# Part of w_o's first rows by GpSimd's queue instead of a half row set aside: one decode step on one core

## The chip, the cores and the metric

The kernel runs on one core of a Trainium2 chip. The metric is the device time of one execution in microseconds (us); the time before is the median of three runs. A profile is one execution recorded by the hardware profiler. Its span goes from the first to the last instruction and is a little shorter than the time of a run.

The core has TensorE (PE, with weight loads as PEld), VectorE (DVE), ScalarE (ACT), GpSimd (POOL) and SyncE (SP), and 16 DMA engines that all of them share. In the kernel, SP issues nearly all transfers.

## The reference

One decode step: attention over a cache and a gated feed-forward block, both fed by the same normalised row, and added.

```python
def _A_ref(x, k_cache, v_cache, wq, wo):          # H, Sk, Dh = 32, 16384, 128; D = 576
    q = (x @ wq).reshape(B, Sq, H, Dh).transpose(0, 2, 1, 3)
    p = _softmax(einsum("bhqd,bhkd->bhqk", q, k_cache) * Dh ** -0.5)
    o = einsum("bhqk,bhkd->bhqd", p, v_cache)
    return o.transpose(0, 2, 1, 3).reshape(B, Sq, H * Dh) @ wo
def _B_ref(x, w_gate, w_up, w_down):              # Df = 4608
    return (_gelu(x @ w_gate) * (x @ w_up)) @ w_down
xn = _layernorm(x)
return x + _A_ref(xn, ...) + _B_ref(xn, ...)
```

All data is float32. K and V of one head are 8 MB each, 32 heads make 537 MB; the weights add 50 MB. Each byte is used once.

## The kernel before, in words

**Order by hand.** `Plan` keeps one list of operations for each engine; `op` and `dma` (L54 to L66) append to it, with the semaphores that the operation waits for. What stands earlier in an engine's list runs earlier on it. `dma` adds 16 to a semaphore when the whole transfer has landed; `then` lets an engine raise a semaphore itself once what it is given has come.

**Stages.** SP loads the three input projections first (w_q, w_gate, w_up, L208 to L300). Then come 32 heads: SP loads K into two buffers in turn and V into one (L405 to L424), VectorE multiplies K by the query and sums, TensorE multiplies by V. SP's list runs ahead: a load is issued as soon as the buffer it overwrites has been read (semaphores `s_kf` for K, `s_vf` for V).

**The end.** With the last heads, free K buffers take the weights of the two output projections. w_down has 36 rows a partition (`FT`), w_o has 32 (`WT`); a "row" here is 576 floats (2304 bytes) in each of 128 partitions, since both are laid out as `(p t) f -> p (t f)`. In SP's list the order is: 28 rows of w_down (L427), the last V (L428), 8 rows of w_down (L429), and then w_o in pieces of 12, 6, 6 and six single rows (`WO_CUTS`, L444 to L449). The first 18 rows of w_o go behind w_down's last 8 into one buffer (`wo0`), free when the last K has been read (`s_kf`, 2). The others wait for VectorE's adds over w_down's first 28 rows (`k_w0`).

Row 31 is split. Its right part (columns 320 to 575, `LEFT` is 320) is loaded early, after the first 18 rows, by eight transfers of 16 KB (L450 to L454): the 128 partitions are laid as two halves beside each other in 64 partitions (`aside`), and one transfer fills eight partitions that are four apart. Row 30 comes in two pieces, right part then left, and the left part of row 31 is last (L456).

**The output.** Attention's 4096 values stand as a column per row of w_o in `oT` (L468). Three routes sum the product into the result:

- VectorE multiplies rows 0 to 10 (`ON_DVE`) by their column and adds them into `wacc`, where w_down's rows and x are already (L470 to L474). Before row 8 it adds the half row set aside, in two halves (L471 to L473); the second needs half of `oT`'s last column moved to the lower partitions (`o31`, L469).
- TensorE sums rows 11 to 25 into `acc` (L491 to L494). VectorE adds `acc` and `wacc` into `part` (L495).
- TensorE sums rows 26 to 31 and `part` over the partitions into one row of results, in three pieces `pair[0]`, `pair[1]` and `third` (L496 to L507). Three copies bring them to `osb`, and SP stores it (L508 to L512).

Of the kernel before, what the change touches and what calls it, by code (L numbers as in the profile page):

```python
# [13 lines left out]
P = 128  # L14
H, SK, DH = 32, 16384, 128
D, DF = 576, 4608
# [7 lines left out]
FT = DF // P  # L24
WT = HD // P
S0 = 32512
SLOT = 4 * N * DH
WD1 = 28
WO1 = 18
# [2 lines left out]
LAST = 6  # L32
SIDE = 160
LEFT = 2 * SIDE
ASIDE = 8
SEL = 396


class Plan:
# [14 lines left out]
    def op(self, e, fn, *deps, sig=None, by=1):  # L54
        if e in ("dve", "act", "pool"):
            deps += (self.last.get(e),)
        sig = sig or self.own[e]
        self.count[sig.name] = self.count.get(sig.name, 0) + by
        self.q[e].append((deps, fn, sig, by))
        if sig is self.own[e]:  # L60
            self.last[e] = sig, self.count[sig.name]
        return sig, self.count[sig.name]

    def dma(self, e, out, in_, *deps, sem=None):
        sem = sem or self.sem(f"d{len(self.count)}")
        return self.op(e, lambda g: g.dma_start(out, in_), *deps, sig=sem, by=16)  # L66
# [65 lines left out]
def plan(nc, pl, x, k_cache, v_cache, wq, wo, wg, wu, wd, out):  # L132
    op, dma = pl.op, pl.dma
# [4 lines left out]
    wov = wo.rearrange("(p t) f -> p (t f)", t=WT)  # L138
# [5 lines left out]
    def small(name, shape, where=None):  # L144
        if where is None:
            size = 4
            for n in shape[1:]:
                size *= n
            where = place[name] = top[0]
            top[0] += -(-size // 32) * 32  # L150
            assert top[0] <= S0, (name, top)
        return nc.alloc_sbuf_tensor_at(name, shape, F32, offset=where).ap()

    def big(name, floats, where):
        assert where + 4 * floats <= 3 * SLOT
        return nc.alloc_sbuf_tensor_at(name, [P, floats], F32, offset=S0 + where).ap()
# [10 lines left out]
    pm, nm, nb, pe = small("pm", [P, 1]), small("nm", [1, 1]), small("nb", [P, 1]), small("pe", [P, N])  # L167
    ls, o4 = small("ls", [P, H + 1]), small("o4", [P, 512])
    oall, oT = small("oall", [P, H + 1]), small("oT", [P, WT])
    o31 = small("o31", [P // 2, 1])  # L170
    gu, hT = small("gu", [P, 2, FT]), small("hT", [P, FT])
    sel = small("tmp", [P, 3 * SEL])
    over = place["tmp"]
# [6 lines left out]
    B, A, C = 0, SLOT, 2 * SLOT  # L180
# [5 lines left out]
    vt = big("vt", N * DH, C)  # L186
    wd0, wd1 = big("wd0", WD1 * D, B), big("wd1", (FT - WD1) * D, A)
    wo0, wo1 = big("wo0", WO1 * D, A + 4 * (FT - WD1) * D), big("wo1", (WT - WO1) * D, B)
    aside = big("aside", 2 * (D - LEFT), A + 4 * (FT - WD1 + WO1) * D)[: P // 2]

    def banks(*shapes):
        with ExitStack() as s:
# [6 lines left out]
    s_hs, s_pm, s_nm, s_p, s_o4, s_v = (pl.sem(n) for n in ("hs", "pm", "nm", "p", "o4", "v"))  # L199
    s_pq, s_pt, s_pb, s_pv, s_pc = (pl.sem(n) for n in ("pq", "pt", "pb", "pv", "pc"))  # L200
    s_qb, s_ol, s_kf, s_vf, s_d, s_a = (pl.sem(n) for n in ("qb", "ol", "kf", "vf", "d", "a"))
    s_kh, s_aside = pl.sem("kh"), pl.sem("aside")
    s_k = [pl.sem(f"k{i}") for i in range(2)]


# [20 lines left out]
    for i in range(2):  # L226
        k = op("dve", lambda g, i=i: g.bn_stats(st[:, i, :], xrow[:, i * HALF : (i + 1) * HALF]), d_x)
    k = op("dve", lambda g: g.bn_aggr(mv, st), k)
    k = op("act", lambda g: g.activation(std, mv[:, 1:2], AF.Sqrt, bias=eps[:1], scale=1.0), k, c_eps)
    k = op("dve", lambda g: g.reciprocal(rstd, std), k)  # L230
# [3 lines left out]
    for j in range(DJ):  # L234
        k = op("pe", lambda g, j=j: g.transpose(px[:, j : j + 1], xm[:, j, :], ones[:1, :1]), k_xn, c_ones)
    k = op("pe", lambda g: g.transpose(px[:, DJ : DJ + 1], xd.rearrange("o d s -> o (d s)"), ones[:1, :1]), k_xd)
    k = op("dve", lambda g: g.tensor_copy(xp, px[:, : DJ + 1]), k)
# [14 lines left out]
    def add(out, w, c, into, *deps):  # L252
        return op("dve", lambda g: g.scalar_tensor_tensor(out, w, c, into, op0=ALU.mult, op1=ALU.add), *deps)  # L253
# [47 lines left out]
    _, g_k, k = rows(gw, gt, d_g, [(0, DF // 4, 0)], lambda: select(qsel, 384, 8, 1))  # L301
# [5 lines left out]
    k = op("act", lambda g: g.activation(qb[0], pqb[:, 0, :DH], AF.Copy), (s_q0, 2))  # L307
# [6 lines left out]
    k = op("pool", lambda g: g.tensor_mul(t1, g_, g_), k_g)  # L314
    k = op("pool", lambda g: g.tensor_scalar(t1, t1, 0.044715, 1.0, op0=ALU.mult, op1=ALU.add), k)
    k = op("pool", lambda g: g.tensor_mul(t1, t1, g_), k)
    k = op("act", lambda g: g.activation(th, t1, AF.Tanh, scale=0.7978845608028654), k)
    k = op("pool", lambda g: g.tensor_scalar(t2, th, 0.5, 0.5, op0=ALU.mult, op1=ALU.add), k)
    k_t = op("pool", lambda g: g.tensor_mul(t2, t2, g_), k)
    k = op("act", lambda g: g.activation(sel.rearrange("p (b c) -> p b c", b=3), pw[:, :, :SEL], AF.Copy), (s_w, 3), k_g, k_t)  # L320
    op("act", lambda g: pick(g, 1), (s_q0, 3), sig=s_hs)
    v = sel[:, : 32 * FT].rearrange("p (r t) -> p r t", r=32)
    k = op("pool", lambda g: g.tensor_mul(v, v, m32[:, :32].unsqueeze(2).to_broadcast([P, 32, FT])), k, c_m32)
    for r in (16, 8, 4, 2, 1):
        o = v[:, :r, :] if r > 1 else u_.unsqueeze(1)
        k = op("pool", lambda g, o=o, r=r: g.tensor_tensor(o, v[:, :r, :], v[:, r : 2 * r, :], op=ALU.add), k)  # L326
    k = op("pool", lambda g: g.tensor_mul(hT, t2, u_), k)
    k = op("pool", lambda g: g.memset(wacc, 0.0), k)
# [104 lines left out]
    o_sum = wacc.rearrange("p a f -> p (a f)")  # L433

    def down(lo, hi, w, dep, k):
        for t in range(lo, hi):
            r, c = w[:, (t - lo) * D : (t - lo + 1) * D], hT[:, t : t + 1]
            k = add(o_sum, r, c, o_sum, dep, k, k_h)
        return k

    k_w0 = down(0, WD1, wd0, d_wd0, None)
    k_w1 = down(WD1, FT, wd1, d_wd1, k_w0)
    d_wo, lo = [], 0
    for n in WO_CUTS:  # L444
        w, base, dep = (wo0, 0, (s_kf, 2)) if lo < WO1 else (wo1, WO1, k_w0)
        c = w[:, (lo - base) * D : (lo - base + n) * D]
        d = dma("sp", c, wov[:, lo * D : (lo + n) * D], dep)
        d_wo += [(c[:, i * D : (i + 1) * D], d) for i in range(n)]
        lo += n  # L449
        if lo == WO1:  # L450
            last = wo.rearrange("(s r t) f -> t r s f", s=2, t=WT)[WT - 1]
            for r in [b + j for b in (0, 32) for j in range(4)]:
                to = aside[r : r + 29 : 4].rearrange("r (s f) -> r s f", s=2)
                d_aside = dma("sp", to, last[r : r + 29 : 4, :, LEFT:], dep, sem=s_aside)  # L454
    assert len(d_wo) == WT - 2
    for t, a, b in ((WT - 2, LEFT, D), (WT - 2, 0, LEFT), (WT - 1, 0, LEFT)):  # L456
        c = wo1[:, (t - WO1) * D + a : (t - WO1) * D + b]
        d_wo.append((c, dma("sp", c, wov[:, t * D + a : t * D + b], k_w0)))


    k = op("pe", lambda g: g.matmul(pqb[:, 0, :H], ones, ls[:, :H], start=True, stop=True))
    k = op("dve", lambda g: g.reciprocal(rl, pqb[:, 0, :H]), k)  # L462
    k = op("dve", lambda g: g.tensor_mul(oexp, oall[:, :H].unsqueeze(2).to_broadcast([P, H, 4]),  # L463
                                         rl.unsqueeze(2).to_broadcast([P, H, 4])), k, k_o)
    k = op("pe", lambda g: g.transpose(pt[:, 0, :P], oexp.rearrange("p h a -> p (h a)"), ident), k)  # L465
    k = op("dve", lambda g: g.tensor_mul(ot, pt[:, 0, :P].rearrange("p (a t) -> p a t", a=4),  # L466
                                         m4.unsqueeze(2).to_broadcast([P, 4, 32])), k, c_m4)
    k_oT = op("dve", lambda g: g.tensor_reduce(oT, ot.rearrange("p a t -> p t a"), axis=AX.X, op=ALU.add), k)  # L468
    k_o31 = op("dve", lambda g: g.tensor_copy(o31, oT[P // 2 :, WT - 1 :]), k_oT)  # L469
    for t in ON_DVE:  # L470
        for i, c in enumerate((oT[: P // 2, WT - 1 :], o31) if t == ASIDE else ()):  # L471
            to = o_sum[: P // 2, LEFT:]
            k_w1 = add(to, aside[:, i * (D - LEFT) : (i + 1) * (D - LEFT)], c, to, d_aside, k_w1, k_o31)  # L473
        k_w1 = add(o_sum, d_wo[t][0], oT[:, t : t + 1], o_sum, d_wo[t][1], k_w1)  # L474


    def row(to, lhs, w, deps, start, stop):
        return op("pe", lambda g: g.matmul(to, lhs, w, start=start, stop=stop), *deps)  # L478

    def whole(at, lhs, w, deps, start, stop):  # L480
        for a in range(2):
            k = row(acc[at : at + 1, a, :HALF], lhs, w[:, a * HALF : (a + 1) * HALF], deps, start, stop)
        return k

    third = fin[64:65, 0, : D - LEFT]
    pair = [fin[32 * i : 32 * i + 1, 0, :SIDE] for i in range(2)]

    def left(lhs, w, deps, start, stop):
        return [row(pair[i], lhs, w[:, i * SIDE : (i + 1) * SIDE], deps, start, stop) for i in range(2)]

    rows = [t for t in range(WT - LAST) if t not in ON_DVE]  # L491
    for i, t in enumerate(rows):
        w, d = d_wo[t]
        k = whole(32 * (i % 4), oT[:, t : t + 1], w, (d, k_oT), i < 4, i >= len(rows) - 4)  # L494
    k_part = op("dve", lambda g: g.tensor_tensor(part, acc[:, :, :HALF], wacc, op=ALU.add), k, k_w1)  # L495
    for t in range(WT - LAST, WT - 2):  # L496
        w, d = d_wo[t]
        row(third, oT[:, t : t + 1], w[:, LEFT:], (d,), t == WT - LAST, False)
        left(oT[:, t : t + 1], w, (d,), t == WT - LAST, False)
        if t == WT - LAST + 1:  # L500
            w = part.rearrange("p a f -> p (a f)")
            row(third, ones[:, 0:1], w[:, LEFT:], (k_part,), False, False)
            left(ones[:, 0:1], w, (k_part,), False, False)
    (w1, d1), (w0, d0), (w, d) = d_wo[WT - 2 :]
    k2 = row(third, oT[:, WT - 2 : WT - 1], w1, (d1,), False, True)
    left(oT[:, WT - 2 : WT - 1], w0, (d0,), False, False)
    k0, k = left(oT[:, WT - 1 :], w, (d,), False, True)  # L507
    to = osb.rearrange("o a f -> o (a f)")  # L508
    c = op("act", lambda g: g.activation(to[:, LEFT:], third, AF.Copy), k2)
    c0 = op("dve", lambda g: g.tensor_copy(to[:, :SIDE], pair[0]), k0)  # L510
# [30 lines left out]
```

## Time and profile before

| | |
|---|---|
| median of three runs | 1362.75 us (1362.43 to 1364.05) |
| span of the profiled execution | 1360.5 us, 6992 instructions |
| bytes read from memory | 587.60 MB |
| busy: PE, DVE, ACT, POOL | 391.3, 1243.5, 66.9, 36.0 us |

The page cuts the span into 40 slices of 34 us. A digit is the busy share of an engine in tenths (9 is 90% or more); the DMA line is the mean over the 16 DMA engines and GB/s is what they moved. Windows cut any stretch in the same way, and there the DMA share has two decimals: one engine that works alone is 1/16 or 0.06. The share can come out a little above 1. The timeline gives the start, the busy time, the engine, the line and the names of an operation; what stands in square brackets is the idle time just before it and what ended it. Queues are named q1, q10 and so on; SP's is q1 and ScalarE's q10; those called "instruction" carry code.

### The profile page before, as it was taken

How to read it: one execution, taken by the hardware profiler on the slowest of the kernel's cores; microseconds unless marked ns; L12 is line 12 of the kernel's file. 1: busy time of each engine (PE TensorE's matmuls, PEld its weight loads, DVE VectorE, ACT ScalarE, POOL GpSimd, SP SyncE). 2: the span in 40 equal slices, each digit the busy share in tenths (PEclk: the TensorE clock that was granted, in tenths of full speed). 3: DMA queues.
4: the chain of work that ended last, by engine and by line, in shares of the span. 5: the costliest groups of instructions: out<-in, count | busy, mean ns of one | idle time of the engine just before them, and what ended most of it. 6: DMA issues, size and time to landing. Idle time of an engine off the chain costs nothing. (4 is left out here: it accounts for less than half of the span.)

```text
span 1360.5 us, 6992 instructions
## 1 busy us (share of the span) xinstructions
PE 391.3 (29%) x2650; PEld 122.4 (9%) x2650; DVE 1243.5 (91%) x228; ACT 66.9 (5%) x234; POOL 36.0 (3%) x25
## 2 busy tenths in 40 slices
PE   0211233333211333333222333332223333322136
PEld 0000011001000111100000111010001111000011
DVE  7999999999988888898888888998888889988888
ACT  0000000000000000000000000000000000000000
POOL 0063000000000000000000000000000000000000
PEclk9655666666556666666556666655666666655667
DMA  9999999999999999999999999999999999999998
GB/s 405 429 437 432 434 447 441 432 432 432 434 432 434 432 432 432 435 451 435 432 432 432 434 432 434 432 432 432 441 447 434 432 432 434 432 434 432 431 432 374
DMA packets 12870, 587.63 MB, mean 432 GB/s; under 512 B 1474, under 2 KB 1986, under 8 KB 2756
## 3 DMA queue, kind: packets, MB, share of 16 engines
q1 hardware_dynamic: 12866, 587.60, 99.8%
q8 instruction: 1, 0.02, 0.0%
q10 hardware_dynamic: 2, 0.00, 0.0%
q14 instruction: 1, 0.01, 0.0%
HBM read 587.60 MB, written 0.00 MB: 432 GB/s over the span
## 5 line engine op out<-in xcount | busy, mean ns | idle before, releaser
L344 PE MATMUL po<-vt,pe 128*4 128x512 f32 x2048 | 291.8, 733 | 611.5 <-PEq L119 611.5
L356 DVE TENSOR_TENSOR kb<-kb,qb 128x16384 f32<-128x16384 f32 (+1 forms) x17 | 277.3, 16314 | 31.8 <-DVEq L119 31.8
L356 DVE TENSOR_TENSOR ka<-ka,qb 128x16384 f32<-128x16384 f32 x16 | 275.6, 17226 | 32.1 <-DVEq L119 32.1
L360 DVE TENSOR_REDUCE sc<-kb 128x128 f32<-128x16384 f32 x16 | 275.5, 17220 | 2.3
L360 DVE TENSOR_REDUCE sc<-ka 128x128 f32<-128x16384 f32 x16 | 275.5, 17220 | 2.3
L344 PEld LDWEIGHTS po<-vt,pe 128*4 128x4 f32 x2048 | 56.3, 98 | 819.9 <-issue 819.9
L337 PE MATMUL pt<-ident,pm 128*1 128x128 f32 x32 | 11.9, 372 | 223.1 <-PEq L119 223.1
L397 ACT ACTIVATE o<-po 128x512 f32<-128x512 f32 x32 | 19.1, 597 | 877.1 <-ACTq L119 877.1
L349 PE MATMUL pc<-m,o 128*128 128x1 f32 x256 | 32.7, 249 | 28.9 <-PEq L119 28.9
L349 PEld LDWEIGHTS pc<-m,o 128*128 128x128 f32 x256 | 31.0, 191 | 57.8 <-issue 57.8
L253 DVE SCALAR_TENSOR_TENSOR wacc<-wd,hT,wacc 128x576 f32<-128x576 f32 x36 | 29.5, 819 | 4.1 <-DMA wd<-in_B_w_down_dram 2.9
L286 PE MATMUL pw<-both,ones 128*32 128x396 f32 x72 | 11.5, 801 | 63.3 <-PEq L119 63.3
L365 DVE TENSOR_REDUCE nm<-pt 1x1 f32<-1x128 f32 x32 | 8.9, 278 | 21.5 <-DVEq L119 21.5
L337 PEld LDWEIGHTS pt<-ident,pm 128*1 128x1 f32 x32 | 2.5, 79 | 228.2 <-issue 228.2
L339 PE MATMUL pb<-nm,ones 1*128 1x1 f32 x64 | 17.7, 343 | 18.5 <-PEq L119 18.5
L339 PEld LDWEIGHTS pb<-nm,ones 1*128 1x128 f32 x64 | 15.9, 307 | 27.8 <-issue 27.8
L393 ACT ACTIVATE nb<-pb 128x1 f32<-128x1 f32 x32 | 5.5, 171 | 254.1 <-ACTq L119 254.1
L363 DVE TENSOR_REDUCE pm<-sc 128x1 f32<-128x128 f32 x32 | 9.2, 286 | 7.6 <-DVEq L119 7.6
L335 PE MATMUL pqb<-qsel,hsel 128*128 128x128 f32 x64 | 14.9, 315 | 1.8 <-PEq L119 1.8
L395 ACT ACTIVATE pe<-sc,nb 128x128 f32<-128x128 f32 x32 | 12.8, 401 | 6.1 <-ACTq L119 6.1
L304 ACT ACTIVATE hsel<-hcol 128x128 f32 (+1 forms) x34 | 10.2, 301 | 41.3 <-DVE qsel L297 41.2
L326 POOL TENSOR_TENSOR tmp<-tmp 128x576 f32<-128x576 f32 (+3 forms) x4 | 11.3, 2836 | 0.3
(93 smaller groups left out, 177.9 us busy)
## 6 DMA issues: line engine op xcount, KB each, us to landing
g<-in_B_w_gate_dram SPq DMA_DIRECT2D x2, 4608.0 KB, 39.5
u<-in_B_w_up_dram SPq DMA_DIRECT2D x2, 4608.0 KB, 32.3
q<-in_A_wq_dram SPq DMA_DIRECT2D x2, 4096.0 KB, 17.4
kb<-in_A_k_cache_dram SPq DMA_DIRECT2D x2, 4096.0 KB, 26.7
wd<-in_B_w_down_dram SPq DMA_DIRECT2D x1, 8064.0 KB, 42.0
wo<-in_A_wo_dram SPq DMA_DIRECT2D x1, 3456.0 KB, 35.9
wo<-in_A_wo_dram SPq DMA_DIRECT2D x2, 1728.0 KB, 28.6
wd<-in_B_w_down_dram SPq DMA_DIRECT2D x1, 2304.0 KB, 28.1
```

What stands on the lines that cost most here:

```text
L253: return op("dve", lambda g: g.scalar_tensor_tensor(out, w, c, into, op0=ALU.mult, op1=ALU.add), *deps)
L286: m = g.matmul(pw[32 * i : 32 * i + 32, b, :SEL], ones[:, :32], bv[:, i, b * SEL : (b + 1) * SEL], start=True, stop=True)
L326: k = op("pool", lambda g, o=o, r=r: g.tensor_tensor(o, v[:, :r, :], v[:, r : 2 * r, :], op=ALU.add), k)
L335: g.matmul(pqb[:, 0, :DH], hsel, qsel, start=True, stop=True).then_inc(s_pq, 1)
L337: g.transpose(pt[:1, 0, :P], pm, ident).then_inc(s_pt, 1)
L339: g.matmul(pb[:, 0, :1], ones[:1, :], nm, start=True, stop=True).then_inc(s_pb, 1)
L344: m = g.matmul(po[q : q + 4, 0, :], pe[:, k : k + 4], vt[:, k * DH : (k + 4) * DH], start=k < 16, stop=k >= N - 16)
L349: m = g.matmul(pc[:, 0, :1], o4[:, j * DH : (j + 1) * DH], m32[:, j : j + 1], start=j == 0, stop=j == 3)
L356: g.tensor_mul(kd, kd, qb[i].unsqueeze(1).to_broadcast([P, n[1] - n[0], DH])).then_inc(s_d, 1)
L360: g.tensor_reduce(sc[i], kt[i].rearrange("p (n d) -> p n d", d=DH), axis=AX.X, op=ALU.add).then_inc(s_d, 1)
L395: g.activation(pe, sc[i], AF.Exp, bias=nb, scale=SCALE, accum_out=ls[:, bass.ds(h, 1)]).then_inc(s_p, 1)
L397: g.activation(o4, po[:, 0, :], AF.Copy).then_inc(s_o4, 1)
```

## The change

Row 31 is no longer set aside: the eight transfers, their buffer, the copy `o31` and the two adds on VectorE go. Row 31's right part is loaded behind row 30's right part, and the two left parts follow; TensorE multiplies it like the others.

The first piece of w_o (12 rows) is issued in parts. SP loads partitions 0 to 111 and then raises `s_go`. GpSimd waits for `s_go` and issues, in its own queue, seven transfers: 8 bytes in each of 4 partitions into a spare buffer `junk`, then partitions 112 to 118, 8 bytes in 1 partition, partitions 119 to 125, 8 bytes in each of 13 partitions, then partition 126 and partition 127 by themselves. When all have landed, GpSimd raises `s_mix`. VectorE's adds of rows 0 to 10 and TensorE's rows 11 to 25 wait for `s_mix` too. The counts 4 + 7 + 1 + 7 + 13 make 32, which is twice the number of DMA engines.

```diff
-ASIDE = 8
+MIX = 112
...
-    o31 = small("o31", [P // 2, 1])
+    junk = small("junk", [P, 6])
...
+    def mixed(c, src, dep):
+
+        d = dma("sp", c[:MIX], src[:MIX], dep)
+        pl.then("sp", [s_go])
+        at, ds = MIX, []
+        for i, (skip, n) in enumerate(((4, 7), (1, 7), (13, 0))):
+            ds.append(dma("pool", junk[:skip, 2 * i : 2 * i + 2], wov[:skip, :2], (s_go, 1)))
+            if n:
+                ds.append(dma("pool", c[at : at + n], src[at : at + n]))
+            at += n
+        ds += [dma("pool", c[p : p + 1], src[p : p + 1]) for p in range(at, P)]
+        pl.then("pool", [s_mix], *ds)
+        return d
+
...
-        d = dma("sp", c, wov[:, lo * D : (lo + n) * D], dep)
+        d = dma("sp", c, src, dep) if lo else mixed(c, src, dep)
...
-        if lo == WO1:
-            last = wo.rearrange("(s r t) f -> t r s f", s=2, t=WT)[WT - 1]
-            for r in [b + j for b in (0, 32) for j in range(4)]:
-                to = aside[r : r + 29 : 4].rearrange("r (s f) -> r s f", s=2)
-                d_aside = dma("sp", to, last[r : r + 29 : 4, :, LEFT:], dep, sem=s_aside)
...
-    for t, a, b in ((WT - 2, LEFT, D), (WT - 2, 0, LEFT), (WT - 1, 0, LEFT)):
-        c = wo1[:, (t - WO1) * D + a : (t - WO1) * D + b]
-        d_wo.append((c, dma("sp", c, wov[:, t * D + a : t * D + b], k_w0)))
+    for a, b in ((LEFT, D), (0, LEFT)):
+        for t in (WT - 2, WT - 1):
+            c = wo1[:, (t - WO1) * D + a : (t - WO1) * D + b]
+            d_wo.append((c, dma("sp", c, wov[:, t * D + a : t * D + b], k_w0)))
...
-        for i, c in enumerate((oT[: P // 2, WT - 1 :], o31) if t == ASIDE else ()):
-            to = o_sum[: P // 2, LEFT:]
-            k_w1 = add(to, aside[:, i * (D - LEFT) : (i + 1) * (D - LEFT)], c, to, d_aside, k_w1, k_o31)
-        k_w1 = add(o_sum, d_wo[t][0], oT[:, t : t + 1], o_sum, d_wo[t][1], k_w1)
+        k_w1 = add(o_sum, d_wo[t][0], oT[:, t : t + 1], o_sum, d_wo[t][1], k_w1, (s_mix, 1))
...
-        k = whole(32 * (i % 4), oT[:, t : t + 1], w, (d, k_oT), i < 4, i >= len(rows) - 4)
+        k = whole(32 * (i % 4), oT[:, t : t + 1], w, (d, k_oT, (s_mix, 1)), i < 4, i >= len(rows) - 4)
...
-    (w1, d1), (w0, d0), (w, d) = d_wo[WT - 2 :]
-    k2 = row(third, oT[:, WT - 2 : WT - 1], w1, (d1,), False, True)
-    left(oT[:, WT - 2 : WT - 1], w0, (d0,), False, False)
-    k0, k = left(oT[:, WT - 1 :], w, (d,), False, True)
+    for i, t in enumerate((WT - 2, WT - 1)):
+        w, d = d_wo[WT - 2 + i]
+        k2 = row(third, oT[:, t : t + 1], w, (d,), False, i == 1)
+    for i, t in enumerate((WT - 2, WT - 1)):
+        w, d = d_wo[WT + i]
+        k0, k = left(oT[:, t : t + 1], w, (d,), False, i == 1)
```

More of the change, by code (lines that the diff above doesn't have):

```diff
@@ L188, in plan @@
     wo0, wo1 = big("wo0", WO1 * D, A + 4 * (FT - WD1) * D), big("wo1", (WT - WO1) * D, B)
-    aside = big("aside", 2 * (D - LEFT), A + 4 * (FT - WD1 + WO1) * D)[: P // 2]
     def banks(*shapes):
@@ L201, in plan @@
     s_qb, s_ol, s_kf, s_vf, s_d, s_a = (pl.sem(n) for n in ("qb", "ol", "kf", "vf", "d", "a"))
-    s_kh, s_aside = pl.sem("kh"), pl.sem("aside")
+    s_kh, s_mix, s_go = (pl.sem(n) for n in ("kh", "mix", "go"))
     s_k = [pl.sem(f"k{i}") for i in range(2)]
@@ L445, in plan @@
         w, base, dep = (wo0, 0, (s_kf, 2)) if lo < WO1 else (wo1, WO1, k_w0)
-        c = w[:, (lo - base) * D : (lo - base + n) * D]
-        d = dma("sp", c, wov[:, lo * D : (lo + n) * D], dep)
+        c, src = w[:, (lo - base) * D : (lo - base + n) * D], wov[:, lo * D : (lo + n) * D]
+        d = dma("sp", c, src, dep) if lo else mixed(c, src, dep)
         d_wo += [(c[:, i * D : (i + 1) * D], d) for i in range(n)]
         lo += n
-        if lo == WO1:
-            last = wo.rearrange("(s r t) f -> t r s f", s=2, t=WT)[WT - 1]
-            for r in [b + j for b in (0, 32) for j in range(4)]:
-                to = aside[r : r + 29 : 4].rearrange("r (s f) -> r s f", s=2)
-                d_aside = dma("sp", to, last[r : r + 29 : 4, :, LEFT:], dep, sem=s_aside)
     assert len(d_wo) == WT - 2
-    for t, a, b in ((WT - 2, LEFT, D), (WT - 2, 0, LEFT), (WT - 1, 0, LEFT)):
-        c = wo1[:, (t - WO1) * D + a : (t - WO1) * D + b]
-        d_wo.append((c, dma("sp", c, wov[:, t * D + a : t * D + b], k_w0)))
+    for a, b in ((LEFT, D), (0, LEFT)):
+        for t in (WT - 2, WT - 1):
+            c = wo1[:, (t - WO1) * D + a : (t - WO1) * D + b]
+            d_wo.append((c, dma("sp", c, wov[:, t * D + a : t * D + b], k_w0)))
     k = op("pe", lambda g: g.matmul(pqb[:, 0, :H], ones, ls[:, :H], start=True, stop=True))
@@ L468, in plan @@
     k_oT = op("dve", lambda g: g.tensor_reduce(oT, ot.rearrange("p a t -> p t a"), axis=AX.X, op=ALU.add), k)
-    k_o31 = op("dve", lambda g: g.tensor_copy(o31, oT[P // 2 :, WT - 1 :]), k_oT)
     for t in ON_DVE:
-        for i, c in enumerate((oT[: P // 2, WT - 1 :], o31) if t == ASIDE else ()):
-            to = o_sum[: P // 2, LEFT:]
-            k_w1 = add(to, aside[:, i * (D - LEFT) : (i + 1) * (D - LEFT)], c, to, d_aside, k_w1, k_o31)
-        k_w1 = add(o_sum, d_wo[t][0], oT[:, t : t + 1], o_sum, d_wo[t][1], k_w1)
+        k_w1 = add(o_sum, d_wo[t][0], oT[:, t : t + 1], o_sum, d_wo[t][1], k_w1, (s_mix, 1))
     def row(to, lhs, w, deps, start, stop):
```

## The prediction

> **What bounds the kernel now.** I began with the page's slices, then read its queue rows and the bytes.
>
> ```profile
> DVE  7999999999988888898888888998888889988888
> DMA  9999999999999999999999999999999999999998
> GB/s 405 429 437 432 434 447 441 432 432 432 434 432 434 432 432 432 435 451 435 432 432 432 434 432 434 432 432 432 441 447 434 432 432 434 432 434 432 431 432 374
> DMA packets 12870, 587.63 MB, mean 432 GB/s; under 512 B 1474, under 2 KB 1986, under 8 KB 2756
> q1 hardware_dynamic: 12866, 587.60, 99.8%
> q10 hardware_dynamic: 2, 0.00, 0.0%
> ```
>
> The DMA row is full in 39 of 40 slices: 587.6 MB at 432 GB/s is 1360 us, the whole span. One engine of sixteen moves 432/16 = 27.0 GB/s. The change moves the same bytes, so only two things can change the time: how evenly the sixteen engines finish, and whether one of them loses time on the way. Nearly everything goes through SP's queue, q1. So next I cut the end into quarters of a microsecond (PE, PEld, DVE, ACT and POOL busy, granted clock, DMA share, GB/s).
>
> ```profile
> 1356.00:1356.25 0.25, 0.25 (x6) 0.00 (x0) 0.25 (x1) 0.00 (x0) 0.00 (x0) 1.00 1.07 389
> 1356.25:1356.50 0.25, 0.17 (x3) 0.00 (x0) 0.25 (x1) 0.00 (x0) 0.00 (x0) 1.00 0.98 358
> 1356.50:1356.75 0.25, 0.18 (x5) 0.13 (x8) 0.02 (x1) 0.00 (x0) 0.00 (x0) 1.00 0.61 223
> 1356.75:1357.00 0.25, 0.25 (x10) 0.19 (x5) 0.00 (x0) 0.00 (x0) 0.00 (x0) 1.00 0.58 213
> 1357.00:1357.25 0.25, 0.25 (x9) 0.08 (x1) 0.00 (x0) 0.00 (x0) 0.00 (x0) 1.00 0.36 127
> 1357.25:1357.50 0.25, 0.25 (x9) 0.16 (x6) 0.00 (x0) 0.00 (x0) 0.00 (x0) 1.00 0.14 51
> 1357.50:1357.75 0.25, 0.25 (x7) 0.10 (x2) 0.00 (x0) 0.00 (x0) 0.00 (x0) 1.00 0.14 51
> 1357.75:1358.00 0.25, 0.25 (x3) 0.08 (x1) 0.00 (x0) 0.00 (x0) 0.00 (x0) 1.00 0.07 26
> 1358.00:1358.25 0.25, 0.25 (x7) 0.09 (x4) 0.00 (x0) 0.00 (x0) 0.00 (x0) 1.00 0.02 5
> ```
>
> A share of 0.14 is 0.14 x 16 = 2.2 engines. So about seven engines stop by 1356.6, seven more by 1357.2, and **two run on alone** to 1357.75 and about 1358.05. These are the two that the change wants to spare. What is left at 1356.25 is the sum of the eight shares times 0.25, 0.72 us; at the full 1.04 it would be gone by 1356.95 instead of 1358.05. **1.1 us is the most that a better balance can give.** What hangs on the last landing is in the timeline:
>
> ```profile
> 1355.76 0.76 DVE L495 TENSOR_TENSOR part<-acc,wacc 128x576 f32<-128x576 f32 x1
> 1358.45 0.09 PEld L478 LDWEIGHTS fin<-wo,oT 128*1 128x1 f32 x4 [0.32 <-DMA wo<-in_A_wo_dram]
> 1359.32 0.28 SPq L66 DMA_DIRECT2D out_dram<-osb  x1
> ```
>
> TensorE waits 0.32 us for the last piece of w_o, so the landing releases the end; from 1358.45 to 1360.5 are 2.05 us that stay. The chain of waits, by contrast, leads through VectorE's adds, which are near the bound but not it. The page has the span, 1360.5 us; the median of the three runs, 1362.75, lies 2.25 us above, and I add that to every sum.
>
> **The change part by part.** *Taken away:* eight transfers of the half row, their two adds, and the copy in front (timeline).
>
> ```profile
> 1309.41 5.89 SPq L66 DMA_DIRECT2D aside<-in_A_wo_dram  x8
> 1344.95 0.15 DVE L469 COPY o<-oT 64x1 f32<-64x1 f32 x1
> 1352.10 0.48 DVE L253 SCALAR_TENSOR_TENSOR wacc<-aside,oT,wacc 64x256 f32<-64x256 f32 x1
> 1352.62 0.48 DVE L253 SCALAR_TENSOR_TENSOR wacc<-aside,o,wacc 64x256 f32<-64x256 f32 x1
> ```
>
> VectorE gets 0.15 + 2 x 0.48 + three gaps of 0.03 = 1.2 us back, but `part` waits for TensorE's rows, and the end for the landing: worth nothing now, though it keeps `part` out of the way if the landing comes 0.9 us earlier. SP's 5.89 us of issuing (1309.4 to 1315.3) lie ahead of its wait for w_down's adds, which ends at 1335.3 (the x10 row below): nothing. The half row's bytes now come at the end as a fourth piece, in SP's queue; the queue's order alters, its sum doesn't.
>
> *Moved:* fourteen partitions of the first twelve rows. A partition's row is 12 x 2304 = 27,648 B, 1.02 us of one engine at 27.0 GB/s. SP's transfer keeps 112 partitions, seven per engine where there were eight; fourteen engines get one back from GpSimd, two don't; the last two partitions are to be split over all. Against an even share the two get 7/8 x 1.02 = 0.9 us less, the others 0.13 us more. The late pair, 0.8 and 1.1 us behind the even end of 1356.95, then ends at about 1356.85 and 1357.15, and the rest between them: **-0.9 us** (bounds 0 and -1.1).
>
> *Added, switching:* GpSimd's queue has seven transfers (three tiny, two of seven rows, two of one). GpSimd itself is idle, and the signal is in time (timeline, and one row of the DMA issues):
>
> ```profile
> 113.77 0.65 POOL L329 COPY wacc<-xrow 1x576 f32<-1x576 f32 x1
> 1303.32 0.34 SPq L66 DMA_DIRECT2D vt<-in_A_v_cache_dram  x1
> 1308.46 0.91 SPq L66 DMA_DIRECT2D wo<-in_A_wo_dram  x2
> 1335.32 14.68 SPq L66 DMA_DIRECT2D wo<-in_A_wo_dram  x10
> 1345.03 0.11 PEld L478 LDWEIGHTS acc<-wo,oT 128*1 128x1 f32 x2 [1.04 <-DMA wo<-in_A_wo_dram]
> ...
> wo<-in_A_wo_dram SPq DMA_DIRECT2D x1, 3456.0 KB, 35.9
> ```
>
> GpSimd starts behind SP's issue at 1308.5, and the rows are wanted at 1345.0. The new waits stand in front of 11 VectorE adds and TensorE's rows; with 36 us of cover they cost nothing unless GpSimd stalls that long. But the transfers run in the middle of V's and w_down's stream. The only foreign transfers in such a stream are two fetches of instructions (first from the stretch 83.3 to 85.6 us, then 141.1 to 142.2):
>
> ```profile
> q14 instruction: 1, 0.01, 0.8%
> ...
> q8 instruction: 1, 0.02, 5.3%
> ```
>
> The second took 5.3% x 16 x 1.1 = 0.93 us for 16,384 B, which at 27.0 GB/s are 0.61: 0.33 us lost. The first took 0.8% x 16 x 2.3 = 0.3 us for 8,192 B: nothing lost. So a foreign packet costs 0 to 0.33 us beside its bytes; seven per engine, 0 to 2.3. The new ones are unlike both in size; I take the middle, **+1.2 us**.
>
> *Added, neighbours:* partitions 112 to 118 and 119 to 125 lie side by side, each written by another engine at the same time, while the stream's own writes go there too. No row of before shows that: its big transfers are 128 partitions wide, and the half row's partitions were four apart (L453). Bounds: side by side, 0; or one after another, where the seventh engine waits 6 x 1.02 = 6.1 us. An engine held up here ends late, and nobody takes its work. Nothing lies nearer to one end, so I take the middle, **+3.1 us**.
>
> [...]
>
> *Added, the two single rows:* 16 pieces of 1,728 B each into one partition. Side by side 0.06 us, one after another 1.02; the middle, 0.5 us, twice: **+1.0 us** (0 to 2.0).
>
> *SP's 112 partitions* I cost at nothing if seven per engine run as eight did; if not, see below.
>
> **Sum:** -0.9 + 1.2 + 3.1 + 1.0 = +4.4; 1360.5 + 4.4 = 1364.9, with 2.25 around it **1367.2 us**, slower by 0.3%. With every term at its end the sum reaches from -1.1 to +10.4; I hold 1364.3 to 1371 for the forecast's own range, since all four ends seldom come together.
>
> **Rivals.**
>
> *It works as it says* (not slower). Foreign packets ride along like the 8 KB fetch, neighbours don't collide: -0.9 + about 0.2 for the tiny pieces, 1362.0 us. For it: the first fetch lost nothing in its own time, and the share stays full around it. Against: the two late engines are late for some reason, the fetches are the only one in sight, and a lag of 0.8 to 1.1 us is more than the 0.3 and 0.93 us that they took. It decides if seven foreign packets per engine and the neighbours together cost under 0.9 us; with that it is faster, by less than 0.1%.
>
> *Switching alone.* Each foreign packet loses 0.33 us, the neighbours don't matter: -0.9 + 2.3 = +1.4, 1364.2 us. For it: the 16 KB fetch.
>
> *SP's transfer collides too.* If 112 partitions are dealt out in other groups than 128, two engines write into the same neighbourhood through seven rows, and each row takes up to twice 1.02 us: 0 to 7.2 us more on the slowest engine. With most of it: 1374 us. For it: it is the same mechanism as in the forecast and 3.1 MB instead of 0.4; against: all 16 engines still have neighbours of their own most of the time. [...]
>
> *It doesn't spare the two.* If a transfer of seven goes to the same seven engines each time, a late engine may get two rows: 1.02 us on top instead of one less, +0.8 instead of -0.9; with the switching +2.0, 1364.7 us. [...]
>
> **How the numbers follow.** Forecast 0.38, works 0.17, switching alone 0.17, SP's transfer too 0.23, not spared 0.05. A measurement of this kernel tells about 0.2%, 2.7 us, from no change (the three runs spread over 1.6 us). Faster by more than that would need 2.7 us where balance has 1.1: 0.01. Slower: the forecast but for its lowest part, 0.35, and 0.23: 0.58. Within: 0.41. The range runs from just under "works", 1361.8, to 1374.0, inside the largest rival; some 0.03 lie below and 0.12 above.
>
> **What would show it.** Balance: the quarter rows fall from full to zero within 0.4 us, no plateau at 0.14. Switching: GB/s dips between 1310 and 1330 by the same amount on all engines. Neighbours: the DMA share in that stretch falls, or some transfers land late one by one and a new plateau of several engines stands at the end, longer than the two of before. SP's transfer: the first w_o load lands later than 35.9 us after issue although it is an eighth smaller. The prediction is wrong if the bytes at the end still stop together: then neighbours cost nothing and the time is about 1362.

## The result and the profile after

The changed kernel takes **1381.25 us** (median of 4 runs, 1380.73 to 1381.53) against 1362.74 before: slower, ratio 1.0136, 95% interval 1.0121 to 1.015. The prediction, 1367.2 in a range up to 1374.0, had the right sign and less than a quarter of the size. The span went from 1360.5 to 1378.6 us, +18.1. First the same rows of the page of the changed kernel:

```profile
DMA  9999999999999999999999999999999999999997
GB/s 411 428 445 428 426 449 430 430 426 453 428 428 432 447 428 428 447 432 430 426 453 428 428 432 447 428 428 447 432 430 426 453 428 428 432 447 428 424 334 252
DMA packets 13030, 587.63 MB, mean 426 GB/s; under 512 B 1604, under 2 KB 2148, under 8 KB 2918
q1 hardware_dynamic: 12802, 587.16, 99.4%
q0 software_dynamic: 224, 0.44, 0.2%
```

The bytes are the same. GpSimd's queue, q0, moved 0.44 MB of them. The DMA row reads 9 in all slices but the last, yet the last two move only 334 and 252 GB/s: the engines count as busy and move little. In windows of 5 us (columns as in the prediction: busy of PE, PEld, DVE, ACT and POOL, granted clock, DMA share, GB/s), first before, then after:

```profile
1315.00:1320.00 5.00, 0.00 (x0) 0.00 (x0) 4.79 (x7) 0.00 (x0) 0.00 (x0) 0.50 0.97 419
1320.00:1325.00 5.00, 0.00 (x0) 0.00 (x0) 4.82 (x6) 0.00 (x0) 0.00 (x0) 0.50 0.97 419
```

```profile
1315.00:1320.00 5.00, 0.00 (x0) 0.00 (x0) 4.82 (x6) 0.00 (x0) 0.00 (x0) 0.50 1.36 366
1320.00:1325.00 5.00, 0.00 (x0) 0.00 (x0) 4.79 (x7) 0.00 (x0) 0.00 (x0) 0.50 0.44 144
1325.00:1330.00 5.00, 0.00 (x0) 0.00 (x0) 4.79 (x7) 0.00 (x0) 0.00 (x0) 0.50 1.06 459
1330.00:1335.00 5.00, 0.00 (x0) 0.00 (x0) 4.79 (x7) 0.00 (x0) 0.00 (x0) 0.50 1.12 260
1335.00:1340.00 5.00, 0.00 (x0) 0.00 (x0) 0.40 (x1) 0.00 (x0) 0.00 (x0) 0.50 0.71 195
1340.00:1345.00 5.00, 4.40 (x32) 0.94 (x36) 0.00 (x0) 0.00 (x0) 0.00 (x0) 0.66 1.06 286
1345.00:1350.00 5.00, 4.10 (x42) 0.88 (x34) 0.08 (x1) 0.60 (x1) 0.00 (x0) 1.00 1.11 251
1350.00:1355.00 5.00, 1.17 (x10) 1.06 (x10) 4.82 (x6) 0.17 (x1) 0.00 (x0) 0.86 0.92 205
1355.00:1360.00 5.00, 0.48 (x1) 0.18 (x1) 2.96 (x7) 0.00 (x0) 0.00 (x0) 0.50 0.95 296
```

The mean of the nine GB/s is 274 over 45 us. At 432 that is 45 x (1 - 274/432) = 16.5 us lost, nearly the whole 18.1. It comes in three troughs: 1315 to 1325 (10 us at 255: 4.1 us), 1330 to 1345 (15 us at 247: 6.4 us) and 1345 to 1360 (15 us at 251: 6.3 us). Shares above 1 stand beside shares far below it, which looks like packets that outlast a window and are counted where they start; so the mean over a trough tells more than any one window. The issues (KB each and us to landing) say what fell into the troughs, first of before, then of after, and below them after's timeline:

```profile
wd<-in_B_w_down_dram SPq DMA_DIRECT2D x1, 2304.0 KB, 28.1
...
vt<-in_A_v_cache_dram SPq DMA_DIRECT2D x32, 28.0
```

```profile
wo<-in_A_wo_dram SPq DMA_DIRECT2D x1, 3024.0 KB, 54.3
wd<-in_B_w_down_dram SPq DMA_DIRECT2D x1, 2304.0 KB, 41.7
wo<-in_A_wo_dram POOLq DMA_DIRECT2D x2, 189.0 KB, 22.8
vt<-in_A_v_cache_dram SPq DMA_DIRECT2D x1, 38.1
```

```profile
1309.37 0.72 POOL L66 DMA_DIRECT2D junk<-in_A_wo_dram  x1 [1194.90 <-SPq L69]
1312.14 1.00 POOL L66 DMA_DIRECT2D wo<-in_A_wo_dram  x2
1349.92 6.80 DVE L252 SCALAR_TENSOR_TENSOR wacc<-wd,hT,wacc 128x576 f32<-128x576 f32 x8 [14.52 <-DMA wd<-in_B_w_down_dram]
1362.86 9.36 DVE L252 SCALAR_TENSOR_TENSOR wacc<-wo,oT,wacc 128x576 f32<-128x576 f32 x11 [4.09 <-DMA wo<-in_A_wo_dram]
1376.54 0.09 PEld L483 LDWEIGHTS fin<-wo,oT 128*1 128x1 f32 x4 [0.31 <-DMA wo<-in_A_wo_dram]
```

GpSimd issued all seven within 4 us. Yet a transfer of 189 KB took 23 us to land, and the bystanders suffer: V's last load took 38.1 us where 28.0 is the median of before; w_down's last eight rows, 41.7 us after 28.1 before; w_o's first piece 54.3 after 35.9, an eighth smaller. VectorE now waits 14.5 us for w_down. The end is as before: TensorE waits 0.31 us for the last landing, and 2.06 us follow. So all of the loss lies in the transfers, and the question is which part of the change does it.

### The profile page after: what moved, and what is told of

The parts are those of the page before. It is cut to its first block, busy times and chain, and to the rows that moved or that the text cites. A ratio compares the mean times of both kernels' runs of the same rounds, so it can differ in the third digit from the quotient of the medians.

```text
span 1378.6 us, 6998 instructions
## 1 busy us (share of the span) xinstructions
PE 392.2 (28%) x2652; PEld 122.6 (9%) x2652; DVE 1242.4 (90%) x225; ACT 66.8 (5%) x234; POOL 39.1 (3%) x32
## 5 line engine op out<-in xcount | busy, mean ns | idle before, releaser
L252 DVE SCALAR_TENSOR_TENSOR wacc<-wd,hT,wacc 128x576 f32<-128x576 f32 x36 | 29.5, 819 | 17.7 <-DMA wd<-in_B_w_down_dram 16.5
L252 DVE SCALAR_TENSOR_TENSOR wacc<-wo,oT,wacc 128x576 f32<-128x576 f32 x11 | 9.0, 819 | 4.4 <-DMA wo<-in_A_wo_dram 4.1
## 6 DMA issues: line engine op xcount, KB each, us to landing
wo<-in_A_wo_dram SPq DMA_DIRECT2D x1, 3024.0 KB, 54.3
wd<-in_B_w_down_dram SPq DMA_DIRECT2D x1, 2304.0 KB, 41.7
```

## The experiments

Two theories at the start. **C**: writers that meet in neighbouring partitions hold each other up, in GpSimd's part, in SP's 112 partitions, or in both. **Q**: GpSimd's transfers in SP's stream cost by themselves, wherever they write. A third came up with the runs own and crossed. **E**: a transfer of seven goes to the same seven engines each time, so that the tiny ones place nothing. A guest, in what follows, is an engine that writes partitions which another engine, the host, writes in SP's transfers of 128 partitions. No trace names the engines: who is a guest is inferred from the time that a row takes.

### tail: without GpSimd's part

```diff
-        d = dma("sp", c[:MIX], src[:MIX], dep)
...
+        return dma("sp", c, src, dep)
```

> The change without its GpSimd part: the first twelve rows of w_o come in one SP transfer of 128 partitions again; the half row stays at the end of the queue. All theories: the span is that of before, 1360.5 us within 0.5, since the same bytes go evenly over the same queue; the late engines end at about 1358.4 as before. If it were over 1365, the cost would lie in the new order of the last pieces and not in the twelve rows.

Span 1360.9; time 0.9996 of before (0.9987 to 1.0006). The other half of the change, the half row back in the queue, costs and gives nothing. It is also the base for what follows.

### own, crossed, close: three places for the same fourteen rows

```diff
+        pl.then("sp", [s_go], dep)
+        ds = []
+        for i, at in enumerate(PLACES):
+            ds.append(dma("pool", c[at], src[at], (s_go, 1)))
+            ds.append(dma("pool", junk[:1, 2 * i : 2 * i + 2], wov[:1, :2]))
+        pl.then("pool", [s_mix], *ds)
+        return dma("sp", c, src, (s_mix, 1))
```

`PLACES` is `(slice(0, 25, 4), slice(64, 89, 4))` in own, the same two exchanged in crossed, and `(slice(112, 119), slice(119, 126))` in close.

> SP loads the twelve rows 128 wide, and ahead of that GpSimd loads fourteen of the same rows as an extra (two transfers of seven, four partitions apart, 0 to 24 and 64 to 88), so that SP's transfer waits for them and writes the same data again. If the seven shares go to engines that write these very partitions in SP's transfers, nobody meets anybody. Theory C (writers that meet in neighbouring partitions hold each other up): one row more for fourteen engines, 1.02 us, span 1361.5 (1361 to 1362.5). Theory Q (a GpSimd transfer in the middle of SP's stream costs by itself, wherever it writes): 5 us or more, 1366 or over.

> As own, with the two lists of partitions exchanged: the first seven shares write 64 to 88, the second 0 to 24, so that each meets one engine that streams there. Theory C: where two meet, each runs at half speed for one row, so an engine loses 1.0 us as a guest and 1.0 us as a host: 1361.5 + 2.0 = 1363.5 (1362.5 to 1365). Theory Q: as own, within 0.5.

> As own, with the partitions of the change, 112 to 118 and 119 to 125, side by side. Theory C: four guests and one host in a group of four partitions; in the changed kernel the first such transfer held all engines up by 3 us and the second by more, so 1361.5 + 6 to 11, 1367.5 to 1372.5. Theory Q: as own, within 0.5.

Spans 1364.0, 1363.7 and 1369.5; times 1.0023 (1.0013 to 1.0034), 1.002 (1.001 to 1.003) and 1.0066 (1.0046 to 1.0086) of before. Same bytes, same queue, same number of transfers, and close is 5.5 us behind own: Q can't explain that. Crossed came out where C had it (1363.5). But own lies 2.5 us above C's 1361.5, and the two are alike, which C did not expect. GpSimd's queue row, cut to the stretch of each transfer of seven, tells why (packets, MB, share of 16 engines). For own, 1312 to 1319 us and 1322 to 1333 us:

```profile
q0 software_dynamic: 34, 0.19, 6.6%
...
q0 software_dynamic: 70, 0.19, 6.4%
```

Of crossed in the same two stretches, and then of close, the first transfer, 1312 to 1319 us:

```profile
q0 software_dynamic: 32, 0.19, 9.7%
...
q0 software_dynamic: 78, 0.19, 4.4%
```

```profile
q0 software_dynamic: 16, 0.19, 17.2%
```

Share x 16 x 7 us is the time of seven rows. Own's first: 7.4 us, 1.06 a row, the 1.02 of a free engine. Own's second: 6.4% x 16 x 11 = 11.3 us, 1.6 a row. Crossed's first: 1.55 a row; its second: 4.4% x 16 x 11 = 7.7 us, 1.1 a row. Close's first: 2.75 a row. So 0 to 24 goes freely and 64 to 88 collides, whichever of them comes first. Had the second seven gone to the engines that write 64 to 88 in SP's transfers, as own was built for, own would have been free in both and crossed in neither. The time of a row grows with the crowd, as C has it: alone 1.06, one guest a place 1.6, seven guests side by side 2.75. The group of four in close's expectation was the author's assumption: these runs have rows four apart and rows side by side, and nothing between. The runs move the source of a row together with its partition, so a collision on the reading side is not excluded by them; but 0 to 24 and 64 to 88 are equally far apart at the source, and only one of them collides.

### home: the tiny transfers of the change, and one home for both

```diff
-        for i, at in enumerate(PLACES):
+        for i, (skip, at) in enumerate(((4, slice(0, 25, 4)), (1, slice(1, 26, 4)), (13, None))):
+            ds.append(dma("pool", junk[:skip, 2 * i : 2 * i + 2], wov[:skip, :2], (s_go, 1)))
...
```

> As own, but with the change's tiny transfers of 4, 1 and 13 partitions around, and the second transfer of seven on 1 to 25 in place of 64 to 88, so that both write partitions that engines 0 to 6 have in SP's transfers. Theory E (a GpSimd transfer of seven goes to the first seven engines each time, and tiny ones before it shift nothing): no engine meets another, the fourteen rows take 7.2 us in each transfer, and seven engines have two rows more, 2 x 1.02, a late one among them: 1360.9 + 2.0 - 0.4 = 1362.5 (1362.2 to 1363.5). Rival (the tiny ones place the shares, as the change assumes): shares on engines 4 to 10 and 12 to 2, guests on the partitions of 0 to 6; 0.9 us lost by all engines in each, rows of 1.3 to 1.7 us, so 1360.9 + 1.0 + 1.8 = 1363.7 or more.

Span 1362.1, time 1.0009 (0.9998 to 1.0021). The two transfers, 1316 to 1323 and 1326 to 1333 us:

```profile
q0 software_dynamic: 46, 0.19, 6.7%
...
q0 software_dynamic: 79, 0.19, 7.0%
```

7.5 and 7.8 us, 1.1 a row: both free. By the change's count the first seven would have been engines 4 to 10, guests in these partitions. **E holds** by these times: with the change's own tiny transfers ahead, both sevens go to the engines that have these partitions in SP's transfers. That those are numbers 0 to 6 was the author's assumption. The placement that the change is built on doesn't happen. Home also says what GpSimd's queue costs where nobody meets: five transfers and 387 KB of extra bytes for 1.2 us, no more than the expected two rows on a late engine. Q is out, and close against home, 1369.5 - 1362.1 = **7.4 us, is the price of the neighbouring partitions** (7.9 by the medians of all runs, of which close has two). Home and close differ in their tiny transfers as well; notiny, below, finds no cost in those.

Whom the neighbours hold up can be read from V's packets of 64 KB in SP's queue: a queue row counts packets by their start, so its share gives the mean time of one. In the changed kernel, 1318 to 1320 us, all seven rows of GpSimd's first transfer start beside nine packets of V, sixteen in all (the other packets of q0 hold 4 bytes each). In home, 1319 to 1321 us, six rows start beside fifteen packets. First the changed kernel, then home:

```profile
q1 hardware_dynamic: 9, 0.59, 152.5%
q0 software_dynamic: 15, 0.19, 60.4%
```

```profile
q1 hardware_dynamic: 15, 0.98, 113.3%
q0 software_dynamic: 15, 0.17, 19.5%
```

A packet of V takes 152.5% x 16 x 2 / 9 = 5.4 us in the changed kernel, each of the nine between 5.3 and 5.7, and 113.3% x 16 x 2 / 15 = 2.4 in home. A partition's 64 KB of V are one packet, so seven partitions have at most seven hosts; at least two of the nine engines write none of them, and they are held up by the same **3.0 us**. The guests' own rows take 60.4% x 16 x 2 / 7 = 2.8 us instead of 1.02. So one such transfer delays all sixteen engines. Beside the second one in close, the core moves 229 and 197 GB/s (1326 to 1330 and 1330 to 1334 us), where tail moves 368 and 415.

### only112 and halves: SP's part

```diff
+        return dma("sp", c[:MIX], src[:MIX], dep)
```

and, for halves,

```diff
+        dma("sp", c[: P // 2], src[: P // 2], dep, sem=s_mix)
+        return dma("sp", c[P // 2 :], src[P // 2 :])
```

> SP's transfer of partitions 0 to 111 alone: nothing by GpSimd, partitions 112 to 127 of the first twelve rows are left out of the load and of the product. Each engine has one row of 27,648 B less, 1.02 us. Theory C with both parts guilty: seven rows per engine no longer fall on the partitions that an engine has in a 128 wide transfer, and in the changed kernel w_o's first piece landed some 6 us late after w_down's: 1360.5 - 1.0 + 6 = 1365.5 (1363 to 1368). If GpSimd's part alone is guilty: 1359.5 within 0.5.

> The twelve rows by two SP transfers, partitions 0 to 63 and 64 to 127, nothing by GpSimd. Theory C (an engine group has its own partitions; 64 neighbouring partitions are home to eight engines only): sixteen engines crowd on the places of eight, half speed for 7.1 MB at 8.2 us: 1360.5 + 8 = 1368.5 (1366 to 1371). If only odd widths such as 112 are bad: 1360.5 within 0.7.

Spans 1365.5 and 1370.5; times 1.0034 (1.0023 to 1.0045) and 1.0065 (1.0042 to 1.0087). Windows in the twelve rows' time, of tail, of only112 and of halves:

```profile
1335.00:1340.00 5.00, 5.00 (x44) 1.02 (x40) 3.94 (x5) 0.00 (x0) 0.00 (x0) 0.89 0.98 424
1340.00:1345.00 5.00, 2.40 (x19) 1.37 (x11) 4.18 (x7) 0.77 (x2) 0.00 (x0) 0.79 0.94 404
```

```profile
1335.00:1340.00 5.00, 5.00 (x48) 1.07 (x40) 2.93 (x5) 0.00 (x0) 0.00 (x0) 0.88 1.07 264
1340.00:1345.00 5.00, 1.99 (x19) 1.37 (x11) 4.43 (x7) 0.77 (x2) 0.00 (x0) 0.80 1.00 265
```

```profile
1335.00:1340.00 5.00, 4.56 (x44) 0.90 (x36) 2.40 (x4) 0.28 (x1) 0.00 (x0) 1.00 0.89 181
1340.00:1345.00 5.00, 1.27 (x10) 1.19 (x10) 4.72 (x7) 0.48 (x2) 0.00 (x0) 0.95 1.19 249
1345.00:1350.00 5.00, 0.48 (x1) 0.18 (x1) 0.98 (x4) 0.00 (x0) 0.00 (x0) 0.50 0.95 194
```

With no GpSimd at all, 112 partitions run at 264 GB/s instead of some 414, and 64 at 208 in the mean, about half, with all engines counted busy. Nearly all bytes there are rows of 27,648 B, which SP's queue row gives a time, first of tail, 1335 to 1340 us, then of only112, 1335 to 1345 us:

```profile
q1 hardware_dynamic: 79, 2.12, 98.3%
```

```profile
q1 hardware_dynamic: 98, 2.65, 103.8%
```

2.12 MB are 77 rows, 98.3% x 16 x 5 / 77 = 1.02 us each; 2.65 MB are 96 rows of 1.7 us. A span of 1365.5 against 1360.9 less one row, 1359.9, makes **5.6 us for SP's 112 partitions**. That is one execution; the eight runs of only112 lie between 1365.90 and 1369.44 us, so the price is good to some 2 us. Halves costs 9.6 us, near the 8.2 that half speed for the 3.5 MB of the twelve rows would make (the expectation's 7.1 MB is a slip, its 8.2 us is not). The third trough of the changed kernel, 6.3 us, is of the size of only112's loss. That the rows of a narrower transfer fall on other engines' places is C's reading of it; which engine writes which row no trace shows. The eight engines that halves' expectation gives to 64 partitions are C's too; the run shows the rate, 208 GB/s.

### singles, nosingles, notiny: the small transfers

```diff
+        ds = [dma("pool", c[p : p + 1], src[p : p + 1], (s_go, 1)) for p in (P - 2, P - 1)]
```

(singles, with the rest as in own), and in the changed kernel

```diff
-        ds += [dma("pool", c[p : p + 1], src[p : p + 1]) for p in range(at, P)]
```

(nosingles) or

```diff
-            ds.append(dma("pool", junk[:skip, 2 * i : 2 * i + 2], wov[:skip, :2], (s_go, 1)))
```

(notiny, with the wait moved to the transfers of seven).

> SP loads the twelve rows 128 wide; ahead of that GpSimd loads partition 126 and partition 127 of them as an extra, by one transfer each, in 16 pieces. If sixteen writers in one partition take turns: up to 1.0 us in each, 1360.9 + 2 = 1362.9. If it is as cheap as in any other place: 1361.0 to 1361.3. Theory C allows for 1361.5 to 1363.

> The changed kernel without the transfers of partitions 126 and 127; these two partitions of the first twelve rows are left out of load and product. The parts so far: without the change's part 1360.9, the two transfers of seven 8.6 less 1.0, SP's 112 partitions 6: 1374.5. If the two single rows make the rest of the 1378.6: 1374.5 (1373.5 to 1375.5). If the rest comes from the parts meeting each other (w_down's rows and w_o's in flight while GpSimd's still land): 1377.5 or more.

> The change without its three tiny transfers. Theory C: the tiny ones cost nothing themselves, but without them the shares of seven go to other engines, and come closer together in time: the span stays within 3 us of 1378.6. If the number of GpSimd's packets were the cost (seven transfers, 18 us, 2.6 us each): 1378.6 - 7.7 = 1371.

Spans 1361.9, 1379.5 and 1380.5; times 1.0008 (0.9997 to 1.0019), 1.0138 (1.0109 to 1.0168) and 1.0144 (1.0114 to 1.0173). The two single rows cost 1.0 us by themselves, and taking them out of the changed kernel saves nothing. Taking out the three tiny ones saves nothing either: neither they nor the number of packets is the cost. Nosingles is 5 us above the sum of the parts as expected, 1374.5, which says that the parts cost more together than alone (only112's share of that sum is good to some 2 us).

### apart: the two colliding parts one after the other

```diff
-        d = dma("sp", c[:MIX], src[:MIX], dep)
-        pl.then("sp", [s_go])
+        pl.then("sp", [s_go], dep)
...
-        return d
+        return dma("sp", c[:MIX], src[:MIX], (s_mix, 1))
```

(on nosingles)

> As nosingles (partitions 126 and 127 of the first twelve rows left out), but SP waits until GpSimd's transfers have landed before it issues its 112 partitions, so that the two colliding parts don't run at the same time. If the parts add up on their own: 1360.9 + 7.6 + 6 = 1374.5 (1373.5 to 1375.5), 5 us less than nosingles' 1379.5, and then what is over in nosingles comes from the parts meeting. If each part simply costs more in this order: as nosingles, 1378 or more.

Span 1377.4, time 1.012 (1.009 to 1.0149): between the two theories. Its last microseconds:

```profile
1369.00:1370.00 1.00, 0.95 (x11) 0.34 (x14) 0.96 (x2) 0.00 (x0) 0.00 (x0) 0.50 0.75 274
1370.00:1371.00 1.00, 1.00 (x16) 0.38 (x12) 0.43 (x1) 0.00 (x0) 0.00 (x0) 0.69 0.17 65
1371.00:1372.00 1.00, 1.00 (x22) 0.55 (x17) 0.00 (x0) 0.00 (x0) 0.00 (x0) 1.00 0.13 49
1372.00:1373.00 1.00, 0.80 (x12) 0.20 (x4) 0.76 (x1) 0.00 (x0) 0.00 (x0) 1.00 0.08 29
1373.00:1374.00 1.00, 0.99 (x17) 0.67 (x18) 0.00 (x0) 0.00 (x0) 0.00 (x0) 1.00 0.07 24
1374.00:1375.00 1.00, 1.00 (x15) 0.39 (x12) 0.00 (x0) 0.00 (x0) 0.00 (x0) 1.00 0.02 9
```

0.13 is two engines, 0.07 is one. Fourteen are done by about 1370.2; two run on, one of them to past 1374. The sum of the parts, a span of 1374.5, nearly holds for the fourteen: with a late pair 1.1 us behind them and the 2.06 us that follow it would be 1373.4. What is over is the pair: 2 and 4 us behind the rest, where before it was 0.8 and 1.1 us behind the even end. The changed kernel ends the same way:

```profile
1371.00:1372.00 1.00, 1.00 (x19) 0.45 (x14) 0.96 (x2) 0.00 (x0) 0.00 (x0) 1.00 0.68 250
1372.00:1373.00 1.00, 1.00 (x19) 0.58 (x15) 0.22 (x1) 0.00 (x0) 0.00 (x0) 1.00 0.44 163
1373.00:1374.00 1.00, 1.00 (x14) 0.20 (x8) 0.63 (x1) 0.00 (x0) 0.00 (x0) 1.00 0.14 51
1374.00:1375.00 1.00, 1.00 (x15) 0.41 (x12) 0.13 (x1) 0.00 (x0) 0.00 (x0) 1.00 0.10 36
1375.00:1376.00 1.00, 1.00 (x10) 0.45 (x10) 0.00 (x0) 0.00 (x0) 0.00 (x0) 1.00 0.07 25
```

So the change lengthened the plateau that it was to remove. That an engine out of step with the others loses more in each collision would explain it; a row too many on a late engine, as E allows, would give 1.0 us of it. How much is which, these runs don't separate.

## Why the prediction was wrong

- **What bounds the kernel**: right. The bytes stayed, VectorE and TensorE only waited, and the loss is in the transfers.
- **Taken away, half row and adds, at nothing**: right (tail, 0.9996).
- **Balance, -0.9**: wrong. The step that took the change's word for the placement failed; the rival "it doesn't spare the two" (0.05) is what happened (home). Its own price had a slip: two rows on a late engine where none was planned make -0.9 + 2 x 1.02 = +1.1, not +0.8.
- **Switching, +1.2**: too much. Home's five transfers cost no more than their bytes; the middle between the two fetches should have been near the end at nothing. The sign set for it, a dip by the same amount on all engines, did come, but from the neighbours. This error and the one in the balance nearly cancel in the sum; that is luck.
- **Neighbours, +3.1**: the mechanism was right and the size less than half of the 7.4 us measured (close against home). One wait was about right: V's packets were held up by 3.0 us. The mis-sized step was "an engine held up here ends late": I charged each engine with one transfer of seven. In fact each of the two held up all sixteen, V's engines that wrote elsewhere too (its packets took 5.4 us beside the first; beside the second in close the core moved 229 and 197 GB/s). So it counts twice, which makes 6.0 of the 7.4.
- **Single rows, +1.0**: the pieces were as counted (GpSimd's queue has 32 packets of 1,728 B in the changed kernel, 16 for each row), the price right alone (singles, 1.0) and not seen in the changed kernel (nosingles).
- **SP's 112 partitions, nothing**: wrong, 5.6 us (only112), and this is the largest error of the sum. I had it as a rival, "SP's transfer collides too", at 0.23 and 1374; its sign came true, 54.3 us to the landing where before took 35.9. What happened was this one together with "not spared", and I had kept them apart as alternatives though nothing made them exclude each other.
- **The sum**: 1360.9 (tail) + 7.4 + 5.6 = 1373.9 of a span of 1378.6. Of the other 4.7, some 3 lie in the first two troughs, which lose 4.1 + 6.4 = 10.5 us where close pays 7.4 (SP's 112 partitions set in towards the end of the second), and more at the end, in the longer plateau. Apart took 2.1 us off nosingles by separating the parts. How much comes from the parts meeting, from the late pair and from the spread of single executions stays open.

The sign was right, because the middle of the bounds for the neighbours pointed up; the range failed, because it held only one of the two collisions at full price.

## What to carry to other kernels

A transfer is more than bytes on a queue: here the partitions that are written at the same time decided whether the engines ran at full speed (spans of 1369.5 us in close, 1362.1 in home). A wide transfer of another shape (112 or 64 partitions, 264 and 208 GB/s), or a second queue's rows in neighbouring partitions (V's packets at 5.4 us instead of 2.4), slowed the whole core. Before balancing engines by a fraction of a row, test with two kernels that differ only in the partitions whether the shares go where they are meant to. And where two mechanisms can both be true, add them up as one case instead of giving each a chance of its own.

## What the runs showed that was not expected

- Guests in a few partitions held up engines that wrote to none of them: with seven rows of 27,648 B in the air, V's packets took 5.4 us instead of 2.4, and the whole core moved 255 GB/s for 10 us (1315 to 1325), where 432 is usual.
- SP's transfer of 112 partitions ran at 264 GB/s with no other queue at work.
- By the time of their rows, GpSimd's transfers of seven went to the same engines twice, with transfers of 4 or 1 partitions in front (home: 1.1 us a row in both).
- Transfers of a few bytes on a second queue, in the middle of a saturated stream, cost nothing that these runs can tell (without the three of the changed kernel the span is 1380.5 us, with them 1378.6; in home they are among the five transfers that cost 1.2 us with all their bytes).
